# The front of a cell-and-feed-forward kernel: a weight converted in ten pieces instead of sixteen, in smaller steps, in another written order

## Chip, core and metric

The kernel runs on one core of a Trainium2 chip, in one launch. The metric is the device time of that launch in microseconds. Three runs of the kernel before gave 463.89, 464.75 and 465.46 us; the median is 464.75 us.

## What is computed

Two blocks follow each other. The first is an mLSTM cell over 4 batches, 8 heads, 768 time steps and a head width of 40; the second is a feed-forward layer with an exact GELU on the 3072 x 320 matrix that the first one gives. The weights arrive in 64-bit floating point.

```python
for t in range(S):                                   # B, H, S, D = 4, 8, 768, 40
    m_new  = maximum(f_gate[t] + m, i_gate[t])
    f_stab = exp(f_gate[t] + m - m_new); i_stab = exp(i_gate[t] - m_new); m = m_new
    C = f_stab * C + i_stab * outer(v[t], k[t])
    n = f_stab * n + i_stab * k[t]
    y[t] = sigmoid(o_gate[t]) * (C @ q[t]) / maximum(abs(n . q[t]), 1)
x = y, laid out as (B*S, H*D)                        # 3072 x 320
h = x @ w_in                                         # w_in 320 x 2048, w_out 2048 x 320
out = (0.5 * h * (1 + erf(h / sqrt(2)))) @ w_out
```

## The kernel before

The 768 steps are cut into 6 chunks of 128. Inside a chunk the cell is written with matrix products: scores (`ps`, L539), weighted by a mask of decays `W`, times the values (`ph`, L657), plus what the state carries in (`pf`, L577 and L582). A chunk has four batches. The feed-forward part takes a chunk's 512 rows at a time: an up product (`pu`, L806 and L812 for chunk 0), GELU on ScalarE (L816), a down product (`po`, L1044 for chunk 0).

The engines run independently and each in the order in which the program issues its instructions. That order is written out by hand in strings. `FRONT` covers the start: chunk 0's cell (small letters), chunk 1's cell (capitals), and chunk 0's feed-forward part. `play` walks through the string word by word; the letter picks a step, the number is its argument. The steps that matter below are these:

- `O n` and `L n` issue loads on SP's queue: `O` the values `vb` and the output gate `ob` of batch n, `L` its keys and queries. Batch numbers run on over the chunks, so `O4` is chunk 1's first batch. `B n` loads a mask tile `W` from DRAM, `M` masks it on GpSimd (L441), `w`/`W` takes its exponential on ScalarE (L467).
- `t`/`T` transposes keys and queries on TensorE (L517); ScalarE copies them out (L520). `T` also weighs chunk 1's values on VectorE (`vw`, L526), which reads `vb`. `c`/`C` is the carried part; for chunk 0 it begins with `vw` on VectorE, then products into a `pf` bank, then a copy of the state on ScalarE (L592). `s`/`S` are the scores and their weighting on VectorE (L542), `v`/`V` the values' products into a `ph` bank, `y`/`Y` the finishing on VectorE (L674 to L679, with a copy `y_rest`, L686), which reads `ph`. `pf` and `ph` share two PSUM banks, tag `h`. `x`/`X` transposes the result for the feed-forward part (L697).
- `A` and `U` are chunk 0's up products for its first and its second half of the rows, four steps each. The second `A` needs weight pieces 3 and 4.
- `F` is one of 16 rows of the down product; row f needs `w_out[:, f, :]`.
- `k n` issues n products that nobody reads, `I n` has the next bank filled with n such products first.
- `K` and `J` convert one piece of a weight from 64 to 32 bits. `K` (`conv_one`): VectorE L371 takes the exponent, ScalarE L373 and L374 turn it into a power of two, VectorE L376 and L378 build the significand. `J` (`conv_two`): VectorE L385 puts in the sign, L388 multiplies and writes the weight; then `fetch(i + 4)` issues the load of the piece four further on into the buffer `bits` of which there are four, so that this load waits in SP's queue until L385 has read the old piece. Ten pieces of 512 columns are `w_in`, then come 16 pieces of 320 columns, one for each row of `w_out`.
- `E` and `N` compute the gates of chunk 1 and of chunks 2 to 5: scans on VectorE, a store of `M` to DRAM on SP, a transpose on TensorE, differences and exponentials.

After `FRONT` come chunk 1's up and down products and so on (`up`, L949 and L960; `down_steps`, L1065), which the change does not touch.

Of the kernel before, what the change touches and what calls it, by code (L numbers as in the profile page):

```python
# [9 lines left out]
F32 = mybir.dt.float32  # L10
F32R = mybir.dt.float32r
BF16 = mybir.dt.bfloat16
U32 = mybir.dt.uint32
# [3 lines left out]
P = 128  # L17
# [8 lines left out]


FRONT = """
    I2 O0 g0 L0 P0 L1 E k1 t0 P1 P2 k7 w0 N k2 w1 O1 K L2 Q s0 O3 w2 q D
    k2 d P3 t1 w3 c0 L3 J v0 t2 K K y0 s1 I7 v1 I8 O2 J g1 L4 I5 c1 K I1  # L30
    I2 y1 s2 x0 t3 B4 O4 B5 g2 J x1 s3 v2 c2 L5 y2 H T0 x2 G0 v3 g3 c3 K y3
    M1 J L6 J A x3 M0 K W0 O7 K A O6 O5 J M2 W1 S0 C0 K J J T1 U U
    K L7 V0 K T2 r J J A G2 K G1 Y0 W2 S1 K M3 C1 A J S2 J K W3 K
    V1 C2 Y1 T3 J J U U S3 V2 K K J G3 J Y2 C3 X0 K V3 J K F J F
    K K B8 F J K F F J K F F F R0 X1 J J K F J F K X2 F J
    K F J Y3 K F R1 e J F Z B9 B10 F X3 R2 Z R3 F p"""
DOWN = """
    F Z M0 Z W0 F M1 L3 W1 S0 C0 M2 F B3 K2 F G1 h0 Q2 D3 G2 V0 K3 Z W2 F Q3 V1 M3 G0 Z F G3 W3 S2 C2 h2 F Y0 F V2
    F Y1 X0 N Y2 F R0 V3 F X1 F Y3 j X2 R1 F R2 X3 R3 F"""
# [3 lines left out]
def kernel(  # L43
# [16 lines left out]
    nc = tc.nc  # L60

    B, H, S, D = q.shape
    L = P
    NCH = S // L
# [4 lines left out]
    DM = H * D  # L69
    DFF = moe_w_in.shape[1]  # L70
    NF = DFF // P
# [6 lines left out]
    WP = 512  # L78
# [5 lines left out]
    raw = ctx.enter_context(tc.tile_pool(name="raw", bufs=2))  # L84
# [14 lines left out]
    w_out = const.tile([P, NF, DM], F32, name="w_out", tag="w_out")  # L99
# [28 lines left out]
    M_d = dram.tile([NCH - 1, BH, L], F32, name="M_d")  # L128
# [3 lines left out]
    def out_of(n):  # L132
        return ob[n % NLD].rearrange("p (h d) -> p h d", d=D)
# [6 lines left out]
    def swapped(c, b):  # L140

        return c > 1 and b % 2 == 1

    def load(n, first=0, end=4):

        if n >= NCH * B:
            return
        c, b = divmod(n, B)
        for src, dst in ((q, qb), (k, kb), (v, vb), (o_gate, None))[first:end]:
            if dst and swapped(c, b):  # L150
                x, to = src[b, :, c * L:(c + 1) * L, :].rearrange("h p d -> p h d"), dst[turn_of(n)][:, :, 0:D]
# [3 lines left out]
            nc.sync.dma_start(out=dst[turn_of(n)][:, :, 0:D] if dst else out_of(n),  # L155
                              in_=src[b, :, c * L:(c + 1) * L, :].rearrange("h p d -> p h d"))
# [19 lines left out]
    def turn_of(n):  # L176

        return n % NLD if n < 2 * B else (n - 2 * B) % NQ
# [35 lines left out]
    a = gates.tile([BH, NCH, L], F32, name="a")  # L214
    M = gates.tile([BH, NCH, L], F32, name="M")
# [58 lines left out]

    def decays_of(e0, e1, g0, g1):

        e, g = slice(e0, e1), slice(g0, g1)
        nc.vector.tensor_tensor(out=ew[:, e], in0=a[:, e], in1=M[:, e, L - 1:L].to_broadcast([BH, e1 - e0, L]),
                                op=OP.subtract)
        nc.vector.tensor_tensor(out=gg[:, g], in0=m0[:, g0 + 1:g1 + 1].unsqueeze(2).to_broadcast([BH, g1 - g0, L]),  # L280
                                in1=M[:, g0 + 1:g1 + 1], op=OP.subtract)
        nc.scalar.activation(out=ew[:, e], in_=ew[:, e], func=AF.Exp)
        nc.scalar.activation(out=gg[:, g], in_=gg[:, g], func=AF.Exp)

    def decays_turned(e0, e1, g0, g1):
        e, g = slice(e0, e1), slice(g0, g1)
        gates_turned((ew[:, e], ewT[:, e]), (gg[:, g], gT[:, g]))
# [21 lines left out]

    def second_gates():  # L310
        gates_of(1, 2)
        nc.sync.dma_start(out=M_d[0], in_=M[:, 1])
        gates_turned((a[:, 1:2], aT[:, 1:2]))
        decays_of(0, 2, 0, 1)

    def later_gates():
        gates_of(2, NCH)
        nc.sync.dma_start(out=M_d[1:].rearrange("c p l -> p c l"), in_=M[:, 2:])
        gates_turned((a[:, 2:], aT[:, 2:]))
        decays_of(2, NCH - 1, 1, NCH - 1)  # L320


    w_src = {}
    for name, w in (("in", moe_w_in), ("out", moe_w_out)):
        rows, cols = w.shape
# [3 lines left out]
    pieces = []  # L329
# [13 lines left out]
    def in_tile(i, x):  # L343

        return w_all[i // 4 * 5 + (2 if x == NX else x + (i % 4) // 2 * 3)]
    for f in range(NF):
        pieces.append(([w_src["out"][f * P:(f + 1) * P, :]], w_out[:, f, :]))
    bits, sig, pow2 = {}, {}, {}

    def fetch(i):  # L350
# [11 lines left out]
    def conv_one(i):  # L362

        if i < len(pieces):
            n = bits[i].shape[1]
            lo, hi = bits[i][:, :, 0], bits[i][:, :, 1]
            s = sig[i] = raw.tile([P, WP], F32, name="sig", tag="sig")[:, 0:n]
            p = pow2[i] = raw.tile([P, WP], F32, name="pow", tag="pow")[:, 0:n]
            su, pu = s.bitcast(U32), p.bitcast(U32)
# [8 lines left out]
            nc.vector.scalar_tensor_tensor(out=s, in0=lo, scalar=2.0 ** -32, in1=su, op0=OP.mult, op1=OP.add)  # L378

    def conv_two(i):  # L380

        if i < len(pieces):
            hi, p = bits.pop(i)[:, :, 1], pow2.pop(i)
            pu = p.bitcast(U32)
            nc.vector.scalar_tensor_tensor(out=pu, in0=hi, scalar=0x80000000, in1=pu,  # L385
                                           op0=OP.bitwise_and, op1=OP.bitwise_or)
            dst, s = pieces[i][1], sig.pop(i)
            nc.vector.scalar_tensor_tensor(out=dst, in0=s, scalar=2.0 ** -20, in1=p, op0=OP.mult, op1=OP.mult)  # L388
            fetch(i + NB)

# [733 lines left out]
    def in_turn(steps):  # L1124
        todo = list(steps)
        return lambda: todo.pop(0)() if todo else None
# [9 lines left out]
    def first_blocks():  # L1136

        copy_chunk(2, range(1))
        for r in (32, 96):
# [2 lines left out]

    first_g = Hidden(False)
    n_pieces = range(len(pieces))
    steps = dict(P=fetch, L=lambda n: load(n, 0, 2), O=lambda n: load(n, 2, 4), B=load_M, E=second_gates, N=later_gates,
                 I=keep_clock, k=warm, D=lambda: decays_turned(0, 2, 0, 1), Q=lambda: decays_turned(2, NCH - 1, 1, NCH - 1),
                 d=lambda: decays_last(0, 1), q=lambda: decays_last(1, NCH - 1), r=halves_out, p=halves_back,
                 A=in_turn(first_up_steps(0)), U=in_turn(first_up_steps(1)), e=first_blocks, F=in_turn(first_down_steps(first_g)),
                 K=in_turn(lambda i=i: conv_one(i) for i in n_pieces), H=products_begin,
                 J=in_turn(lambda i=i: conv_two(i) for i in n_pieces), Z=split_weight)  # L1150
    steps |= cell_steps(0, "mwgtscvyx") | cell_steps(1, "MWGTSCVYXR")
    play(FRONT, steps)
    for c in range(1, NCH):
# [6 lines left out]
        steps = cell_steps(c + 1, "MWGTscVYXRLKQDCBSjh", g)  # L1160
# [36 lines left out]
```

## Time and profile before

| | us |
|---|---|
| median of three runs | 464.75 |
| profiled execution, its own time | 465.24 |
| its span in the profile | 463.2 |
| TensorE busy | 452.3 (98%) |
| VectorE busy | 336.7 (73%) |
| ScalarE busy | 253.0 (55%) |
| GpSimd busy | 79.0 (17%) |
| chunk 0's first up product starts / chunk 0's down product starts / chunk 1's up product starts | 40.8 / 93.5 / 128.8 |

The 2.0 us between the span and the execution's own time lie around the program. Times in the text below are those of the profile, from the start of the span. In a line of the timeline the first number is the start, the second the duration, and where idle time came before an instruction it stands in brackets with what ended it. VectorE's instructions overlap a little, so the step from one start to the next is what counts in a sum; it is up to 0.1 us shorter than the duration.

### The profile page before, as it was taken

How to read it: one execution, taken by the hardware profiler on the slowest of the kernel's cores; microseconds unless marked ns; L12 is line 12 of the kernel's file. 1: busy time of each engine (PE TensorE's matmuls, PEld its weight loads, DVE VectorE, ACT ScalarE, POOL GpSimd, SP SyncE). 2: the span in 40 equal slices, each digit the busy share in tenths (PEclk: the TensorE clock that was granted, in tenths of full speed). 3: DMA queues.
4: the chain of work that ended last, by engine and by line, in shares of the span. 5: the costliest groups of instructions: out<-in, count | busy, mean ns of one | idle time of the engine just before them, and what ended most of it. 6: DMA issues, size and time to landing. Idle time of an engine off the chain costs nothing.

```text
span 463.2 us, 13002 instructions
## 1 busy us (share of the span) xinstructions
PE 452.3 (98%) x5348; PEld 400.5 (86%) x5348; DVE 336.7 (73%) x737; ACT 253.0 (55%) x545; POOL 79.0 (17%) x120
## 2 busy tenths in 40 slices
PE   8899999999999999999998999999999999999996
PEld 7687888867788899988898998899998899988996
DVE  7899879798868996746577654587664685699950
ACT  6986999854354784203694113594123594257701
POOL 3002120000020232300443200353301411200000
PEclk9999999999999999999999999999999999999999
DMA  9997993268777650057972056973049960210001
GB/s 168 203 215 184 199 224 105 64 135 226 111 201 153 120 98 5 24 115 149 200 124 33 11 118 139 208 112 61 1 87 172 164 106 3 79 38 0 1 1 57
DMA packets 174875, 51.11 MB, mean 110 GB/s; under 512 B 154752, under 2 KB 168352, under 8 KB 174816
## 3 DMA queue, kind: packets, MB, share of 16 engines
q1 hardware_dynamic: 174496, 49.95, 52.9%
q8 instruction: 42, 0.69, 0.6%
q10 hardware_dynamic: 320, 0.33, 0.2%
q14 instruction: 17, 0.14, 0.1%
HBM read 45.47 MB, written 10.03 MB: 120 GB/s over the span
## 4 chain that ended last, share of the span: by engine, by line
PE 89%; DVE 4%; DMA 2%; SPq 1%; POOL 1%; issue 1%; ACT 0%; DVEq 0%; POOLq 0%
PE po L1065 25%; PE pu L949 23%; PE po L1044 7%; PE pu L806 6%; PE pu L960 6%; PE po L919 6%; PE ph L657 4%; PE ps L555 3%; PE pu L812 2%; PE px L697 2%; PE pf L610 1%; PE ps L539 1%; SPq L155 1%; PE pf L577 1%; PE pt L517 1%
## 5 line engine op out<-in xcount | busy, mean ns | idle before, releaser
L1065 PE MATMUL po<-w_out,g 128*128 128x160 f32 x512 | 76.2, 303 | 0.0
L964 ACT ACTIVATE g<-pu 128x512 f32<-128x512 f32 x64 | 32.2, 618 | 77.4 <-PE pu L960 77.4
L1065 PEld LDWEIGHTS po<-w_out,g 128*128 128x128 f32 x512 | 70.3, 190 | 2.2 <-ACT g L964 1.3
L467 ACT ACTIVATE W<-W,aT 128x128 f32<-128x128 f32 x128 | 39.2, 389 | 2.1 <-POOL W L441 2.0
L949 PE MATMUL pu<-x_hi,w_in_hi 128*128 128x512 f32 x160 | 39.0, 387 | 0.0
L441 POOL TENSOR_SCALAR_AFFINE_SELECT W<-W 128x1024 f32<-128x1024 f32 (+2 forms) x20 | 25.0, 1258 | 79.1 <-DMA W<-M_d 70.4
L949 PE MATMUL pu<-x_lo,w_in_lo 128*128 128x512 f32 x160 | 37.8, 379 | 0.0
L1065 PE MATMUL po<-w_sums,sums 128*128 128x160 f32 x256 | 36.9, 302 | 0.0
L1065 PEld LDWEIGHTS po<-w_sums,sums 128*128 128x128 f32 x256 | 35.0, 190 | 0.4
L1044 PE MATMUL po<-w_out,g 128*128 128x320 f32 x128 | 35.2, 433 | 0.0
L686 ACT COPY y_rest<-ob 128x128 f32<-128x128 f32 x16 | 4.8, 298 | 55.4 <-DVE ob L679 29.2
L949 PEld LDWEIGHTS pu<-x_hi,w_in_hi 128*128 128x128 f32 x160 | 29.5, 189 | 5.7 <-ACT g L964 1.3
L949 PEld LDWEIGHTS pu<-x_lo,w_in_lo 128*128 128x128 f32 x160 | 30.2, 189 | 4.3
L526 POOL TENSOR_TENSOR vw<-vb,ewT 128x328 f32<-128x328 f32 x12 | 9.2, 780 | 138.4 <-DMA vb<-in_v_dram 99.2
L1044 PEld LDWEIGHTS po<-w_out,g 128*128 128x128 f32 x128 | 24.0, 190 | 9.6
L949 PE MATMUL pu<-x_all,w_mid 128*128 128x512 f32 x80 | 30.3, 379 | 0.0
L949 PE MATMUL pu<-x_all,w_in_mid 128*128 128x512 f32 x80 | 30.3, 379 | 0.0
L806 PE MATMUL pu<-first_x,w_in 128*128 128x256 f32 x128 | 28.9, 381 | 0.0
L793 DVE TENSOR_TENSOR sums<-g 128x512 f32<-128x512 f32 x16 | 13.6, 853 | 18.3 <-ACT g L964 18.3
L806 PEld LDWEIGHTS pu<-first_x,w_in 128*128 128x128 f32 x128 | 23.8, 190 | 3.3 <-DVE w_in L388 0.2
L765 DVE TENSOR_TENSOR w_in_mid<-w_in_hi,w_in_lo 128x512 fp32r<-128x512 f32 x20 | 13.7, 686 | 16.5 <-PE pu L949 16.5
L561 DVE TENSOR_TENSOR W<-ps,W 128x256 f32<-128x256 f32 (+1 forms) x48 | 17.9, 413 | 10.7 <-PE ps L555 9.0
(196 smaller groups left out, 963.2 us busy)
## 6 DMA issues: line engine op xcount, KB each, us to landing
W<-M_d SPq DMA_DIRECT2D x16, 512.0 KB, 5.6
bits<-in_moe_w_in_dram SPq DMA_DIRECT2D x20, 256.0 KB, 4.5
bits<-in_moe_w_out_dram SPq DMA_DIRECT2D x16, 320.0 KB, 3.2
blocks<-kq_d SPq DMA_DIRECT2D x32, 128.0 KB, 3.3
ob<-in_o_gate_dram SPq DMA_DIRECT2D x24, 160.0 KB, 4.4
out_dram<-o_sb SPq DMA_DIRECT2D x36, 80.0 KB, 2.0
kq_d<-in_k_dram SPq DMA_DIRECT2D x32, 80.0 KB, 2.5
kq_d<-in_q_dram SPq DMA_DIRECT2D x32, 80.0 KB, 2.5
```

What stands on the lines that cost most here:

```text
L441: nc.gpsimd.affine_select(out=x, in_=x, compare_op=OP.is_ge, fill=1.0e30, base=base, pattern=[[0, H], [1, x.shape[2]]], channel_multiplier=-1)
L467: nc.scalar.activation(out=W[n][:, h, :], in_=src, func=AF.Exp, scale=-1.0, bias=aT[:, self.c, r:r + 1])
L555: nc.tensor.matmul(ps[i][hip][halves[x ^ i], p, t], kT[i][r, p, halves[x]], qT[i][r, p, t], start=True, stop=True)
L561: nc.vector.tensor_tensor(out=w[r, :, t], in0=ps[i][hip][r, :, t], in1=w[r, :, t], op=OP.mult)
L657: nc.tensor.matmul(ph[r, h, :], Pm[:, h, r], vb[turn_of(n)][:, h, :], start=True, stop=True)
L806: nc.tensor.matmul(banks[-1][e][:, i - i0, :], in_tile(i, x)[:, e, i % 2 * P:(i % 2 + 1) * P], first_x[:, x, t0:t1], start=(x == 0 and i = ...
L919: nc.tensor.matmul(in_pairs(po[t]), x[:, t * L:(t + 1) * L], in_turns(w), start=(f, k) == first, stop=(f, k) == last, skip_group_check=True)
L949: nc.tensor.matmul(in_pairs(pus[i][e]), w[k][:, e, i * P:(i + 1) * P], in_turns(x[:, k, :]), start=(n == 0 and k == 0), stop=False, skip_g ...
L960: nc.tensor.matmul(in_pairs(pu[e]), w[r, i // 2, i % 2 * P:(i % 2 + 1) * P], in_turns(x[r, NX, :]), start=False, stop=(n == 2), skip_group ...
L964: nc.scalar.activation(out=g.t[:, HF * e + i, :], in_=pu[e], func=AF.Gelu, scale=4097.0)
L1044: nc.tensor.matmul(po[b], g.t[:, f, b * L:(b + 1) * L], w_out[:, f, :], start=(f == 0), stop=(f == NF - 1))
L1065: nc.tensor.matmul(bank[k][:, t, :], lhs(j, t), rhs(j), start=(first and t == 0 and j == 0), stop=(t == 1 and j == HF - 1), skip_group_che ...
```

## The change

`w_out` is converted as one run of 5120 columns, cut into ten pieces of 512 instead of sixteen of 320. A piece then holds parts of two or three rows of `w_out`, and its load is issued as two or three DMAs, 24 in all instead of 16. `K` keeps L371 and the two ScalarE operations; L376 and L378 become a step `b` (`conv_sig`). `J` keeps L385; L388 and the fetch become a step `f` (`conv_out`). `E` and `N` are taken apart into `a` (scans), `o` (store), `n` (transpose) and `l` (decays). The string is written anew:

```diff
 FRONT = """
-    I2 O0 g0 L0 P0 L1 E k1 t0 P1 P2 k7 w0 N k2 w1 O1 K L2 Q s0 O3 w2 q D
-    k2 d P3 t1 w3 c0 L3 J v0 t2 K K y0 s1 I7 v1 I8 O2 J g1 L4 I5 c1 K I1
-    I2 y1 s2 x0 t3 B4 O4 B5 g2 J x1 s3 v2 c2 L5 y2 H T0 x2 G0 v3 g3 c3 K y3
-    M1 J L6 J A x3 M0 K W0 O7 K A O6 O5 J M2 W1 S0 C0 K J J T1 U U
-    K L7 V0 K T2 r J J A G2 K G1 Y0 W2 S1 K M3 C1 A J S2 J K W3 K
-    V1 C2 Y1 T3 J J U U S3 V2 K K J G3 J Y2 C3 X0 K V3 J K F J F
-    K K B8 F J K F F J K F F F R0 X1 J J K F J F K X2 F J
-    K F J Y3 K F R1 e J F Z B9 B10 F X3 R2 Z R3 F p"""
+    I2 O0 g0 L0 P0 L1 E l0,2,0,1 t0 o1,2 P1 w0 a2,6 P2 k7 o2,6 n l2,5,1,5 k3 w1 O1 K b L2 Q s0 O3 w2 q D k2 d
+    P3 t1 w3 c0 b L3 J f v0 t2 K b y0 s1 K I7 O2 J f v1 g1 L4 I5 c1 K b I1 I2 y1 s2 x0 t3 B4 J x1 f s3 v2 v3
+    O4 B5 g2 c2 L5 y2 H T0 x2 G0 g3 c3 K b J f y3 L6 J M1 f A x3 M0 K b W0 O7 K b A O6 O5 J f M2 W1 S0 C0 K b
+    J f J f T1 U U K b L7 V0 K b T2 r J f J f A G2 K b G1 Y0 W2 S1 K b M3 J C1 A f S2 J f K b K b V1 C2 Y1 T3
+    J f W3 J U U S3 V2 K f b K b J f G3 J f Y2 C3 X0 K b V3 J K b F J f f F K b K b B8 F J f F F J f F F F R0
+    X1 F F X2 F F Y3 F R1 e F F Z B9 X3 Z B10 R2 R3 F p"""
...
-    for f in range(NF):
-        pieces.append(([w_src["out"][f * P:(f + 1) * P, :]], w_out[:, f, :]))
+    cuts = sorted({*range(0, NF * DM, DM), *range(0, NF * DM + 1, WP)})
+    for n in range(0, NF * DM, WP):
+        rows = [(c // DM, c % DM, d - c) for c, d in zip(cuts, cuts[1:]) if n <= c < n + WP]
+        pieces.append(([w_src["out"][f * P:(f + 1) * P, 2 * c:2 * (c + w)] for f, c, w in rows],
+                       w_out.rearrange("p f d -> p (f d)")[:, n:n + WP]))
...
+    def conv_sig(i):
+        if i < len(pieces):
+            lo, hi = bits[i][:, :, 0], bits[i][:, :, 1]
+            s = sig[i] = raw.tile([P, WP], F32, name="sig", tag="sig")[:, 0:bits[i].shape[1]]
+            su = s.bitcast(U32)
             nc.vector.tensor_scalar(out=su, in0=hi, scalar1=0xFFFFF, scalar2=0x100000,
                                     op0=OP.bitwise_and, op1=OP.bitwise_or)
             nc.vector.scalar_tensor_tensor(out=s, in0=lo, scalar=2.0 ** -32, in1=su, op0=OP.mult, op1=OP.add)
...
+    def conv_out(i):
+        if i < len(pieces):
+            dst, s, p = pieces[i][1], sig.pop(i), pow2.pop(i)
+            bits.pop(i)
             nc.vector.scalar_tensor_tensor(out=dst, in0=s, scalar=2.0 ** -20, in1=p, op0=OP.mult, op1=OP.mult)
             fetch(i + NB)
```

In the third line of the old string and the second and third of the new one, three moves stand out: `v3` goes from behind `T0 x2` to right behind `v2`; `O4 B5` goes from ahead of the third `J` to behind that piece's `f` and behind `s3 v2 v3`; and one `K` goes behind `s1`.

More of the change, by code (lines that the diff above doesn't have):

```diff
@@ L311, in second_gates, with store_M, later_turned @@
         gates_of(1, 2)
-        nc.sync.dma_start(out=M_d[0], in_=M[:, 1])
         gates_turned((a[:, 1:2], aT[:, 1:2]))
[L314 to L318, printed above, removed]
+    def store_M(c0, c1):
+        nc.sync.dma_start(out=M_d[c0 - 1:c1 - 1].rearrange("c p l -> p c l"), in_=M[:, c0:c1])
+    def later_turned():
         gates_turned((a[:, 2:], aT[:, 2:]))
-        decays_of(2, NCH - 1, 1, NCH - 1)
     w_src = {}
@@ L364, in conv_one @@
         if i < len(pieces):
[L365 to L369, printed above, removed]
+            hi = bits[i][:, :, 1]
+            p = pow2[i] = raw.tile([P, WP], F32, name="pow", tag="pow")[:, 0:bits[i].shape[1]]
+            pu = p.bitcast(U32)
             nc.vector.tensor_scalar(out=pu, in0=hi, scalar1=20, scalar2=0x7FF,
@@ L382, in conv_two @@
         if i < len(pieces):
-            hi, p = bits.pop(i)[:, :, 1], pow2.pop(i)
-            pu = p.bitcast(U32)
+            hi, pu = bits[i][:, :, 1], pow2[i].bitcast(U32)
             nc.vector.scalar_tensor_tensor(out=pu, in0=hi, scalar=0x80000000, in1=pu,
                                            op0=OP.bitwise_and, op1=OP.bitwise_or)
-            dst, s = pieces[i][1], sig.pop(i)
+    def conv_out(i):
+        if i < len(pieces):
+            dst, s, p = pieces[i][1], sig.pop(i), pow2.pop(i)
+            bits.pop(i)
             nc.vector.scalar_tensor_tensor(out=dst, in0=s, scalar=2.0 ** -20, in1=p, op0=OP.mult, op1=OP.mult)
@@ L1144 @@
     n_pieces = range(len(pieces))
-    steps = dict(P=fetch, L=lambda n: load(n, 0, 2), O=lambda n: load(n, 2, 4), B=load_M, E=second_gates, N=later_gates,
+    steps = dict(P=fetch, L=lambda n: load(n, 0, 2), O=lambda n: load(n, 2, 4), B=load_M, E=second_gates, n=later_turned,
+                 a=gates_of, o=store_M, l=decays_of,
                  I=keep_clock, k=warm, D=lambda: decays_turned(0, 2, 0, 1), Q=lambda: decays_turned(2, NCH - 1, 1, NCH - 1),
@@ L1149 @@
                  K=in_turn(lambda i=i: conv_one(i) for i in n_pieces), H=products_begin,
-                 J=in_turn(lambda i=i: conv_two(i) for i in n_pieces), Z=split_weight)
+                 J=in_turn(lambda i=i: conv_two(i) for i in n_pieces), b=in_turn(lambda i=i: conv_sig(i) for i in n_pieces),
+                 f=in_turn(lambda i=i: conv_out(i) for i in n_pieces), Z=split_weight)
     steps |= cell_steps(0, "mwgtscvyx") | cell_steps(1, "MWGTSCVYXR")
```

## The prediction

> **What bounds the kernel now.** I read the page first: TensorE is busy for 98% of the span, VectorE for 73%. Then I asked for the busy time by stretch, to see where TensorE's missing 2% lie.
>
> ```profile
> PE 452.3 (98%) x5348; PEld 400.5 (86%) x5348; DVE 336.7 (73%) x737; ACT 253.0 (55%) x545; POOL 79.0 (17%) x120
> ```
> ```profile
> 46.00:68.00 22.00, 22.00 (x219) 18.50 (x219) 17.15 (x33) 21.72 (x41) 3.91 (x4) 1.00 1.02 224
> 68.00:72.00 4.00, 4.00 (x59) 3.31 (x58) 3.83 (x11) 3.97 (x8) 0.37 (x1) 1.00 0.56 162
> 72.00:92.00 20.00, 20.00 (x306) 17.41 (x304) 16.56 (x43) 18.57 (x38) 0.00 (x0) 1.00 0.25 70
> 92.00:94.00 2.00, 1.56 (x68) 1.17 (x67) 1.91 (x6) 1.94 (x4) 0.00 (x0) 1.00 0.00 0
> 94.00:129.00 35.00, 35.00 (x138) 24.87 (x136) 29.80 (x80) 16.59 (x32) 1.04 (x1) 1.00 0.77 165
> ```
>
> The columns are the stretch, its length, then busy time with instruction counts of PE, PEld, DVE, ACT and POOL. From 46 us on TensorE idles 0.44 us up to 129 us, at full clock (1.00), and the down product runs evenly: in the chain of waits 64 of L1044's matmuls take 17.42 us and 40 take 10.77, 0.27 each. So a shift of the point where this unbroken stretch begins comes out at the end one to one, and nothing saved on another engine behind that point comes out at all. Who sets the point? The waits of PEld between 46 and 130 us name one edge, and the timeline shows it:
>
> ```profile
> PEld pu L806 <- DVE w_in L388: 0.2, 1, 0.2
> ```
> ```profile
> 38.84 0.49 DVE L526 TENSOR_TENSOR vw<-vb,ewT 128x328 f32<-128x328 f32 x1
> ...
> 40.44 1.46 DVE L378 SCALAR_TENSOR_TENSOR sig<-bits,sig 128x512 f32<-128x512 uint32 x1
> ...
> 45.56 0.69 DVE L388 SCALAR_TENSOR_TENSOR w_in<-sig,pow 128x512 f32<-128x512 f32 x1
> ...
> 45.88 3.72 PE L806 MATMUL pu<-first_x,w_in 128*128 128x256 f32 x16
> ```
>
> The second A starts at 45.88 and its second matmul needs weight piece 4, which VectorE finishes at 46.25. VectorE has worked almost without a pause since 3.5 us, so **the kernel's length is set by when VectorE finishes piece 4**; after that TensorE sets it. Two more things of this stretch matter: when loads are issued, and how long they take to land.
>
> ```profile
> 30.56 1.62 SPq L191 DMA_DIRECT2D W<-M_d  x1
> 32.27 0.39 SPq L155 DMA_DIRECT2D vb<-in_v_dram  x1
> 32.76 0.52 SPq L155 DMA_DIRECT2D ob<-in_o_gate_dram  x1
> 33.33 2.96 SPq L191 DMA_DIRECT2D W<-M_d  x1
> 36.39 1.68 SPq L359 DMA_DIRECT2D bits<-in_moe_w_in_dram  x2
> ```
> ```profile
> 40.19 2.66 POOL L441 TENSOR_SCALAR_AFFINE_SELECT W<-W 128x1024 f32<-128x1024 f32 x2 [34.90 <-DMA W<-M_d]
> ```
> ```profile
> blocks<-in_q_dram SPq DMA_DIRECT2D x1, 160.0 KB, 4.2
> ```
> ```profile
> qb<-in_q_dram SPq DMA_DIRECT2D x1, 160.0 KB, 5.6
> ```
> ```profile
> vb<-in_v_dram SPq DMA_DIRECT2D x1, 160.0 KB, 5.1
> ```
>
> The last three are the DMA issues of short windows: at 29.50 and 45.38 a 160 KB load right behind two loads of a piece, and O4's `vb` at 32.27.
>
> **The change part by part.** I add to the profiled execution, 465.24 us (span 463.2 and 2.04 around it), and carry the shift to the median, 464.75.
>
> *Ten pieces.* By start-to-start steps a 320-column piece costs VectorE 0.23+0.35+0.41+0.52+0.41 = 1.92 us and a 512-column one 0.33+0.46+0.61+0.72+0.61 = 2.73; 16 x 1.92 - 10 x 2.73 = 3.4 us saved. ScalarE: 16 x (0.557+0.562) - 10 x (0.720+0.722) = 3.5 us saved. All of it lies behind 69.9 us, where the first w_out piece begins, beside an unbroken TensorE: 0 on the path. Per piece ScalarE takes 0.32 longer; four come before the last GELU of chunk 0 ends (90.66), which makes it some 92, and the down product starts at 93.5: covered with 1.5 us to spare, beyond which it would count in full. All conversion ends after about the sixth F row (some 107 us instead of 125); each row has its columns early. The 8 more DMAs cost SP 8 x 0.33 = 2.6 us of issue in a stretch in which it spends 28 us on eight issues, waiting for L385: 0.
>
> *Gates in two parts.* VectorE's, ScalarE's and SP's orders stay what they were (scans, store, transpose copy, differences, exponentials, then piece 0). Only `w0`'s products go ahead of seven unread ones, so ScalarE's wait of 1.37 us at 11.42 ends, but it then waits for the differences, as now, until 13.76. 0. One unread product less before `t0`, one more before `w1`: 0.
>
> *Conversion in smaller steps, up to piece 4.* The same VectorE instructions stand before the end of piece 4 in both orders, so only its pauses can change. One `K` (L371) behind `s1` brings W(s1) forward by 0.3, but its ScalarE pair and the table load behind it move to 27.5, `g1` ends at 30.8 instead of 29.5 and `y1` starts 0.2 late. The pause ahead of the last scores (0.49, ScalarE's copies of `t3`) stays. So `y2` runs from 37.26 instead of 37.14: +0.1.
>
> *v3 forward.* It needs W(s3), done at 36.85, so it fills TensorE's 0.72 us pause at 37.28. But now `v2` and `v3` hold both banks of tag `h`, and `c2` must wait until `y2` has read its own, 38.0: about when `v3` is through. `c2`, `T0`, `x2`, `c3` would give the first A at 40.6, against 40.78. Small either way, as piece 4 decides.
>
> *O4 and B5 behind the third piece's fetch.* Here I see the cost. That fetch waits for L385 of piece 2, at 34.4 (33.63 to 34.31 now). SP, free at 32.2, stands still for 2.2 us, then issues two loads of 256 KB (1.2 us), and `vb` of O4 goes out at 35.65 instead of 32.27. `T0`'s `vw` reads it and stands on VectorE at 38.96, ahead of `c3`'s `vw`, pieces 3 and 4 and `y3`. Landing: 4.2 to 5.6 us after the issue by the two nearest rows, both a 160 KB load behind two pieces; I take 5.0, near the row of this same load, hence 40.65. VectorE waits 40.65 - 38.96 = 1.7 us (0.9 to 2.3). Queued behind it: everything to piece 4, and `c3` on TensorE.
>
> *GpSimd's masks.* The L378 at 40.44 took 1.46 instead of 0.69 while the first mask ran: 0.77 us of the present path. B5 now goes out at some 36.6 and lands some 2.8 us after `vb`, near 43.4; the masks then meet piece 3's L385 or L388. I take 0.7 again (0 if they fall into `y3`, whose input is in PSUM and which was not stretched at 41.83; 1.5 if both masks hit).
>
> The Trainium skill (SBUF — State Buffer, "Who interferes with whom") calls this port an exclusive lock that a VectorE instruction with two SBUF inputs shares with a GpSimd one that reads SBUF; by it the whole mask is the price, 1.2 us, if the mask starts first, and the sum would be 0.5 us higher; this row shows 0.77.
>
> *The sum.* Without either, piece 4 would end at 46.25 - 0.77 + 0.1 = 45.6. With them 45.6 + 1.7 + 0.7 = 48.0, a shift of 1.75, say 1.7. The later order changes (`W3` behind `T3`, the last `X3` one DMA earlier, the rest of F) leave TensorE's list as it was: 0. Profiled execution 466.9, **median 466.4**. Ends: 45.6 + 0.9 = 46.5 (+0.25) and 45.6 + 2.3 + 1.5 = 49.4 (+3.15), so 465.0 to 467.9.
>
> **The rivals.**
>
> *The load is in time; nothing changes.* If `vb` lands by 38.96, 3.3 us after its issue, the wait is 0 and only the mask's 0.7 stays: 45.6 + 0.7 = 46.3, that is 464.8. For it: early loads on an empty queue land that fast (`vb` issued at 1.63 has landed by 4.5). Against: the B mask tile ahead is 512 KB and lands at 36.5. The Trainium skill (DMA: Bandwidth & Descriptors, "Anatomy of one DMA") gives 2.0 us plus bytes over 436 GB/s, an estimate of 2.4 us for 160 KB, by which the load is in time; every load of that size between 20 and 50 us took 4.2 us or more.
>
> *Faster: the small steps win what they can.* The load is in time, the masks fall into `y3`, and the second A starts as soon as TensorE is there: 45.6, or -0.65; the lighter engines also remove TensorE's two pauses behind (0.44 at 92.9; 16 matmuls of L539 at 68.7 take 1.43 instead of 0.89 us). -0.65 - 0.44 - 0.54 = -1.6: 463.1. Against it: the profile puts both pauses down to issue, to no engine that is made lighter.
>
> *Slower by more: the banks.* If `c3`'s bank is the one that `v3` holds, `c3` on TensorE waits for `y3`, which stands behind piece 3's conversion: `y3` has read at some 45.7, `c3` and the first A (4.8 us) then push the second A to 51.4, +5.4: 470.2. Against it: `c2`'s bank is free by then, its state being copied at 39.2.
>
> **How the numbers follow.** Forecast 0.58, load in time 0.21, faster 0.13, banks 0.08. A measurement here tells 0.3% (1.4 us) from no change. Of the forecast's spread (+0.25 to +3.15, centre 1.7) some two thirds lie above 1.4: 0.40, and with the banks 0.48 slower. Its lower third and the load in time give 0.18 + 0.21 = 0.39 the same; 0.13 faster. The range takes in both near rivals partly and the top end with a little more: 463.9 to 468.3.
>
> **What would show it.** In the profile after: SP issues `vb` of O4 at 35 to 36 us, behind the two `bits` loads; L526 on VectorE shows a wait of 1 to 2 us for the DMA of `vb` near 39; the masks start near 43 and one VectorE instruction of piece 3 is stretched; the second A starts near 47.5 and the down product near 95.3, the last with no pause between its rows; VectorE's busy time falls by about 3.4 us and ScalarE's by 3.5. I am wrong if `vw` does not wait, if the second A starts before 46, if TensorE pauses between 50 and 129, or if the down product waits for a `w_out` piece.

## The result

| | before | after |
|---|---|---|
| median, same chip, six runs each | 465.23 us (463.89 to 466.88) | 470.01 us (469.09 to 471.81) |
| profiled execution / its span | 465.24 / 463.2 | 470.9 / 469.1 |

The ratio is 1.0099, with a 95% interval of 1.0071 to 1.0126: slower by some 4.8 us. The prediction said slower, by 1.7 us, with an upper end of 468.3; the time lies above that end. The page of the kernel after begins:

```profile
PE 454.0 (97%) x5348; PEld 401.9 (86%) x5348; DVE 334.7 (71%) x707; ACT 249.8 (53%) x533; POOL 80.3 (17%) x120
```

VectorE is busy for 2.0 us less (forecast 3.4) and ScalarE for 3.2 us less (forecast 3.5), TensorE for 1.7 us more (its granted clock was 0.79 between 248 and 256 us). The stretches again, columns as before:

```profile
46.00:68.00 22.00, 21.79 (x222) 18.21 (x219) 16.71 (x30) 20.98 (x39) 4.61 (x4) 1.00 0.96 221
68.00:72.00 4.00, 3.75 (x30) 2.68 (x29) 3.93 (x8) 3.29 (x7) 0.00 (x0) 1.00 0.48 67
72.00:92.00 20.00, 19.30 (x239) 16.70 (x238) 19.32 (x46) 18.97 (x36) 0.00 (x0) 1.00 0.35 109
92.00:94.00 2.00, 2.00 (x99) 1.82 (x97) 1.22 (x3) 1.99 (x4) 0.00 (x0) 1.00 0.98 290
94.00:98.00 4.00, 2.24 (x84) 1.78 (x79) 3.93 (x10) 3.41 (x6) 0.00 (x0) 1.00 0.34 104
98.00:133.00 35.00, 35.00 (x138) 24.86 (x136) 21.75 (x49) 11.45 (x20) 1.03 (x1) 1.00 0.68 126
```

TensorE now has holes where it had none, 0.25 us between 68 and 72 and 0.70 between 72 and 92, and just ahead of the down product it stands for 1.76 us instead of 0.44. (The 0.21 that is missing between 46 and 68 is the second `A`, which waits for piece 4.) The waits between 37 and 130 us name the holes (total, count, longest):

```profile
PE ph L663 <- issue: 1.8, 1, 1.8
...
DVE vw L532 <- DMA vb<-in_v_dram: 1.3, 1, 1.3
PE pf L583 <- DVE vw L532: 1.2, 1, 1.2
...
PE pf L583 <- DVE state L603: 0.7, 1, 0.7
...
PE ps L545 <- ACT kT L526: 0.2, 1, 0.2
```

The second and the third are the forecast wait and its echo on TensorE. The first was 0.44 us before; the last two are new. Set side by side at points of TensorE's fixed order, the two profiles give this account:

| TensorE starts | before | after | shift | added since the row above |
|---|---|---|---|---|
| S0 (L539, now L545) | 50.49 | 52.05 | 1.56 | 1.56: forecast as 1.7 |
| C1 (L577, now L583) | 70.24 | 72.26 | 2.02 | 0.46 |
| C2 | 77.78 | 80.58 | 2.80 | 0.78 |
| down product (L1044, now L1050) | 93.53 | 97.65 | 4.12 | 1.32 |
| up product of chunk 1 | 128.83 | 132.96 | 4.13 | 0.01 |

From there to the end this profile takes 336.1 us, that of before 334.4. The same stretch took 332.5 to 336.2 us in the profiles of all the kernels told of here, without order, so I read nothing from it; the medians, 4.8 us apart, leave 0.7 us for it.

**The forecast part** is there line by line (issue on SP, then VectorE, GpSimd and TensorE):

```profile
35.29 0.38 SPq L153 DMA_DIRECT2D vb<-in_v_dram  x1
```
```profile
40.30 0.50 DVE L532 TENSOR_TENSOR vw<-vb,ewT 128x328 f32<-128x328 f32 x1 [1.32 <-DMA vb<-in_v_dram]
...
43.25 1.47 DVE L394 SCALAR_TENSOR_TENSOR w_in<-sig,pow 128x512 f32<-128x512 f32 x1
...
47.12 0.69 DVE L394 SCALAR_TENSOR_TENSOR w_in<-sig,pow 128x512 f32<-128x512 f32 x1
```

The load goes out at 35.29, 5.0 us later `vw` may start, GpSimd's mask begins at 43.08 and stretches one instruction of piece 3, and piece 4 is done at 47.81, where I had 48.0.

**The first unforecast part** lies on VectorE and GpSimd, 64 to 67 us. After, and then before:

```profile
63.69 1.39 DVE L532 TENSOR_TENSOR vw<-vb,ewT 128x328 f32<-128x328 f32 x1
65.00 1.02 DVE L367 TENSOR_SCALAR pow<-bits 128x512 uint32<-128x512 uint32 x1
65.93 1.25 DVE L378 TENSOR_SCALAR sig<-bits 128x512 uint32<-128x512 uint32 x1
```
```profile
63.27 1.45 POOL L447 TENSOR_SCALAR_AFFINE_SELECT W<-W 128x1024 f32<-128x1024 f32 x1 [8.01 <-ACT qT L526]
64.78 2.12 POOL L1146 MEMSET blocks<- 32x1024 f32 x2
```
```profile
65.45 1.46 DVE L378 SCALAR_TENSOR_TENSOR sig<-bits,sig 128x512 f32<-128x512 uint32 x1
66.84 0.49 DVE L526 TENSOR_TENSOR vw<-vb,ewT 128x328 f32<-128x328 f32 x1
67.25 0.68 DVE L385 SCALAR_TENSOR_TENSOR pow<-bits,pow 128x512 uint32<-128x512 uint32 x1
```
```profile
65.18 1.19 POOL L441 TENSOR_SCALAR_AFFINE_SELECT W<-W 128x1024 f32<-128x1024 f32 x1 [8.23 <-DVE pow L371]
66.43 1.94 POOL L1140 MEMSET blocks<- 32x1024 f32 x2
```

Before, the fourth mask stretched one instruction (1.46 for 0.69) and the two memsets that follow it on GpSimd met `vw` and L385, which kept their times. After, the mask stretches `vw` (1.39 for 0.49) and the memsets meet two TENSOR_SCALARs, which take 1.02 and 1.25 instead of 0.42 each: 2.3 us in all instead of 0.8. VectorE is then late for ScalarE, which waits 0.67 us for L367 ahead of its copies of T2's keys, and for the state that C2 reads. Here is the last addition to that state and C2's first product, before and then after:

```profile
75.89 0.32 DVE L597 TENSOR_TENSOR state<-state,pf 128x164 f32<-128x164 f32 x1
...
77.78 0.67 PE L577 MATMUL pf<-vw,kb 128*64 128x41 f32 x16
```
```profile
80.10 0.33 DVE L603 TENSOR_TENSOR state<-state,pf 128x164 f32<-128x164 f32 x1
...
80.58 0.67 PE L583 MATMUL pf<-vw,kb 128*64 128x41 f32 x16 [0.70 <-DVE state L603]
```

**The second** is the pause inside V3, ahead of the down product, which both profiles put down to "issue":

```profile
93.31 0.28 PE L657 MATMUL ph<-v,W 128*32 128x41 f32 x8 [0.44 <-issue]
```
```profile
97.44 0.28 PE L663 MATMUL ph<-v,W 128*32 128x41 f32 x7 [1.76 <-issue]
```

### The profile page after: what moved, and what is told of

Its sections match the earlier page's. It is cut to its first block, busy times and chain, and to the rows that moved or that the text cites. A ratio compares the mean times of both kernels' runs of the same rounds, so it can differ in the third digit from the quotient of the medians.

```text
span 469.1 us, 12974 instructions
## 1 busy us (share of the span) xinstructions
PE 454.0 (97%) x5348; PEld 401.9 (86%) x5348; DVE 334.7 (71%) x707; ACT 249.8 (53%) x533; POOL 80.3 (17%) x120
## 4 chain that ended last, share of the span: by engine, by line
PE 75%; DVE 8%; DMA 6%; ACT 4%; SPq 2%; issue 2%; POOL 2%; POOLq 0%; DVEq 0%; ACTq 0%
PE pu L955 22%; PE po L1071 21%; PE po L1050 7%; PE po L925 6%; PE pu L966 5%; PE ph L663 3%; PE pu L812 2%; PE ps L561 2%; DMA vb<-in_v_dram 2%; PE px L703 2%; ACT W L473 1%; PE pf L616 1%; SPq L153 1%; POOL W L447 1%; DMA W<-M_d 1%
## 5 line engine op out<-in xcount | busy, mean ns | idle before, releaser
L1050 PE MATMUL po<-w_out,g 128*128 128x320 f32 x128 | 35.2, 433 | 0.0
L1050 PEld LDWEIGHTS po<-w_out,g 128*128 128x128 f32 x128 | 24.0, 190 | 9.6
```

The source lines that it names most:

```text
L1050: nc.tensor.matmul(po[b], g.t[:, f, b * L:(b + 1) * L], w_out[:, f, :], start=(f == 0), stop=(f == NF - 1))
```

## The experiments

The table compares all of them; each ratio is taken against runs of the kernel before on the same chip. "S0 to down" is the time from TensorE's S0 to the start of the down product. A shift of TensorE ahead of S0 drops out of it, but a late S0 gives the other engines more lead (b_load). "C2" and "V3" are the two pauses.

| kernel | ratio to before | C2 | V3 | S0 to down |
|---|---|---|---|---|
| before | | 0 | 0.44 | 43.04 |
| after | 1.0099 [1.0071, 1.0126] | 0.70 | 1.76 | 45.60 |
| b_load | 1.0034 [1.0013, 1.0055] | 0 | 0.22 | 42.48 |
| a_load | 1.0054 [1.0007, 1.0100] | 0.70 | 1.49 | 44.75 |
| b_ten | 1.0050 [1.0032, 1.0068] | 0 | 1.75 | 44.71 |
| b_B8 | 1.0006 [0.9986, 1.0025] | 0 | 0.63 | 43.07 |
| b_more | 1.0091 [1.0060, 1.0121] | 0 | 2.02 | 44.29 |
| b_hold | 1.0020 [0.9998, 1.0042] | 0 | under 0.15 | 42.77 |
| a_mem | 1.0054 [1.0034, 1.0074] | 0 | 1.26 | 43.66 |
| a_hold | 1.0062 [1.0042, 1.0081] | 0.71 | 0.76 | 44.59 |
| a_c1 | one run, 465.96 beside 463.71 us | 0 | 1.40 | 43.91 |
| a_fix | 0.9993 [0.9979, 1.0007] | 0 | 0.31 | 42.58 |
| a_best | 1.0057 [1.0035, 1.0079] | 0 | 0.71 | 45.60 |
| a_after4 | 0.9994 [0.9978, 1.0011] | 0 | 0.39 | 43.08 |

### b_load: the kernel before, O4 and B5 moved alone

```diff
-t3 B4 O4 B5 g2 J x1 s3 v2 c2
+t3 B4 g2 J x1 s3 v2 O4 B5 c2
```

> The kernel before with one move: O4 and B5 go from ahead of the third J to behind it (and behind s3 and v2), nothing else. Theory A (the late load of vb is what shifts piece 4): vb of O4 is issued at about 35.5 instead of 32.3, T0's vw on VectorE waits 1.0 to 1.8 us for it near 39, the second A starts its second matmul at 47.3 to 48.0 instead of 46.2, and chunk 0's down product starts 1.0 to 1.8 us later than in the kernel before (93.5). Rival (the shift comes from the split steps or from v3): vw does not wait or the wait is swallowed, and the down product starts within 0.4 us of 93.5.

```profile
40.31 0.50 DVE L526 TENSOR_TENSOR vw<-vb,ewT 128x328 f32<-128x328 f32 x1 [1.39 <-DMA vb<-in_v_dram]
```

The wait is 1.39 us, the second A stands until 48.14, and the down product starts at 94.81, 1.28 later than before. The move alone makes the wait and costs the time, a ratio of 1.0034. That step of the prediction holds.

### a_load: the kernel after, O4 and B5 ahead of the third J again

```diff
-t3 B4 J x1 f s3 v2 v3 O4 B5 g2 c2
+t3 B4 O4 B5 J x1 f s3 v2 v3 g2 c2
```

> The changed kernel with that move alone taken back: O4 and B5 stand ahead of the third J again. Theory A: vb is issued near 32.5, vw does not wait, piece 4 is done at 45.6 to 46.4 instead of 47.8, and the start of the down product (97.65 in the changed kernel) comes 1.3 to 3 us earlier, the upper end if the GpSimd collisions of 63 to 67 us move away with it. Rival: the load is only the first of several late things, and the down product still starts later than 97.0, because the masks or the state of chunk 1 take its place.

```profile
38.86 0.49 DVE L532 TENSOR_TENSOR vw<-vb,ewT 128x328 f32<-128x328 f32 x1
...
40.47 1.56 DVE L380 SCALAR_TENSOR_TENSOR sig<-bits,sig 128x512 f32<-128x512 uint32 x1
...
41.95 1.57 DVE L386 SCALAR_TENSOR_TENSOR pow<-bits,pow 128x512 uint32<-128x512 uint32 x1
```

`vw` no longer waits, but now both early masks meet a piece, at 0.87 and 0.88 us, so the second A ends only 0.5 earlier. The waits of C2 and V3 stay. The down product starts at 96.33, 1.3 earlier, at the low end of what was expected; 2.8 of the 4.1 us stay. By the ratio about half of the loss stays, with a wide interval.

### b_ten: the kernel before, with the ten pieces alone

```diff
-    for f in range(NF):
-        pieces.append(([w_src["out"][f * P:(f + 1) * P, :]], w_out[:, f, :]))
+    cuts = ...   # the ten runs of 512 columns, as in the change
```

> The kernel before with w_out in ten pieces of 512 columns and nothing else (its ten K, J pairs left over do nothing). Theory A: up to the first up products nothing changes; from 70 us on a K or J takes longer (2.73 instead of 1.92 us of VectorE for a piece), so chunk 1's states come later and a wait of up to 0.7 us may show ahead of C2 near 78; the down product starts at 93.4 to 94.6. Rival (longer pieces are the main loss behind 68 us): it starts at 95.5 or later. What the prediction said: 93.5, no change.

```profile
95.00 0.28 PE L660 MATMUL ph<-v,W 128*32 128x41 f32 x8 [1.75 <-issue]
```
```profile
90.00:92.00 2.00, 2.00 (x100) 1.79 (x96) 1.82 (x5) 1.99 (x5) 0.00 (x0) 1.00 0.92 310
```

With the old order and nothing else changed, the down product starts 1.68 us late, at 95.21, between the two cases expected; C2 does not wait. Of the 1.68, 1.31 is the pause inside V3. The other 0.37 lies ahead of C3: the longer pieces make ScalarE late (it copies T3's queries at 88.35 instead of 86.70), and the weight load of S3 waits 0.50 us for that copy. This is the edit that I had put at 0. What differs from before at that point is the traffic: DMA share 0.92 between 90 and 92 us, where it was 0.03. Two pieces are now five loads, issued from 88.0 to 90.3 us (the two loads of before went out at 85.5 and 86.9) and landing until 95.0, and in the trace TensorE's next 16 KB of instructions come in their midst, from 92.07 to 93.56. The page lists the queue that they come in (packets, MB, share of the DMA engines' time):

```profile
q8 instruction: 42, 0.69, 0.6%
```

That they are TensorE's is inferred. Each kernel has 42 packets of 16 KB in this queue, against 10,696 matmuls and weight loads, 255 to a packet; all other instructions of the span are some 2,300. The pause stands at a fixed place of TensorE's list: behind 56 of V3's 64 products in the kernels with the old order, behind 57 in those with the new one. And behind 30 us the 14 profiles told of here have 39 pauses of TensorE that are put down to "issue": all stand among products of 41 columns, and each ends 1.1 to 1.7 us after such a packet has landed (those in V3 1.1 to 1.5). The profile itself says only "issue". b_B8, b_more, b_hold and a_hold test what traffic does to it.

### b_B8: the kernel before, the 512 KB load of B8 moved to 87.3 us

```diff
-U U S3 V2 ... K K B8 F J K F
+U U S3 B8 V2 ... K K F J K F
```

> The kernel before with the 512 KB load of B8 issued right behind the scores S3 (near 88 us) instead of behind the second F (near 103), so that data moves while TensorE's next instructions are loaded near 91 us. Theory B (the pause inside V3 is TensorE waiting for its instructions, and data traffic stretches it): the pause of 0.44 us inside V3 grows to 1 to 2 us, the 16 KB instruction load near 91 us takes longer or starts later, and the down product starts 0.6 to 1.6 us later. Rival (the pause in the changed kernel has another cause, such as VectorE's W): it stays between 0.3 and 0.6 us.

```profile
93.51 0.28 PE L657 MATMUL ph<-v,W 128*32 128x41 f32 x8 [0.63 <-issue]
```
```profile
90.00:92.00 2.00, 2.00 (x93) 1.82 (x79) 2.00 (x5) 0.89 (x3) 0.00 (x0) 1.00 0.36 111
```

The pause grew by 0.19 only, and the time did not change. By what was expected that speaks for the rival. But the load was nearly through when the packet came: the DMA share was 0.36, not 0.92. So the test was too weak, and the next makes it stronger.

### b_more: the kernel before, with four more loads at that time

```diff
+    spare = dram.tile([4, P, WP], U32, name="spare")
+    def spare_loads():
+        for n in range(4):
+            nc.sync.dma_start(out=spare[n], in_=w_src["out"][n * P:(n + 1) * P, 0:WP])
...
-T3 J J U U S3
+T3 J J z U U S3
```

> Left as it is: the kernel before, 16 pieces, its own order. Added: four loads of 256 KB from w_out to a scratch place in DRAM, issued right behind the two fetches that follow T3 (at 87.4 us before), which nobody reads. TensorE's instructions are those of the kernel before up to the down product. Theory (TensorE's next 16 KB of instructions come through the same DMA engines as the data, and the loads that are under way at 91 us hold them up): the instruction packet takes 1.3 us or more instead of 1.10 or starts late, the pause inside V3 is 1.2 to 1.9 us instead of 0.44, and the down product starts at 94.3 to 95.0 instead of 93.5. Rival (the longer pause has to do with the other program, not with traffic): pause 0.2 to 0.6, down product at 93.4 to 93.7. Second rival (the number of DMAs counts, not their bytes; these are four, the ten-piece kernels have five small ones): pause in between, 0.6 to 1.2.

```profile
98.94 0.28 PE L663 MATMUL ph<-v,W 128*32 128x41 f32 x8 [2.02 <-issue]
```
```profile
94.00:96.00 2.00, 2.00 (x95) 1.85 (x83) 2.00 (x5) 1.07 (x3) 0.00 (x0) 1.00 0.89 240
```

Four loads that nobody reads, and the pause is 2.02 us: traffic alone makes it, with 16 pieces. All starts here are some 4 us later than before because TensorE ran at a granted clock of 0.50 from 16 to 24 us in this profiled execution; S0 to the down product leaves that out. The ratio is larger than the pause explains, but six of the seven runs had a mean granted clock of 0.985 to 0.996, where three of 32 runs of before had 0.996 or less on that chip. The seventh, at 0.999, took 465.44 us, 1.2 more than the median of before there (464.26), which is what S0 to the down product shows. Why the clock was lower in the other six stays open.

### b_hold: ten pieces, two of their fetches held back

```diff
-T3 J J U U S3 V2 K K J G3 J            # these two J fetch pieces 16 and 17
+T3 J J U U S3 V2 K K z16 z17 J G3 J    # z: a memset of one column of bits on VectorE, then the fetch
```

> The kernel before with the ten w_out pieces alone, but the loads of pieces 16 and 17 held back until VectorE has begun two more pieces (a memset of one column on VectorE ahead of each load, behind the K K that follow V2): they go out at 94 to 95 us instead of 88 to 90.5, so nothing is loaded while TensorE fetches its instructions at 91 to 93.5. Theory (traffic holds the instructions up): the pause inside V3 falls from 1.75 to 0.2 to 0.7, and the down product starts at 93.8 to 94.3 instead of 95.2 (0.26 of the ten pieces' delay ahead of S3 and 0.1 behind it stay). Time 465.5 to 466.5 beside 467.7. Rival (not the traffic at that time): pause 1.5 to 1.9, down product at 95.0 to 95.4, time 467.5.

```profile
93.06 1.16 PE L663 MATMUL ph<-v,W 128*32 128x41 f32 x64
```
```profile
90.00:92.00 2.00, 2.00 (x98) 1.82 (x96) 1.83 (x3) 1.99 (x4) 0.00 (x0) 1.00 0.05 12
```

The same ten pieces with nothing loaded at 90 to 92 us: V3's 64 products run through without a pause, and from S0 to the down product it takes 42.77 us instead of b_ten's 44.71. (S0 itself is 0.9 late here, as both early masks met piece 4: 1.31 and 1.46 us for 0.42 and 0.69.) The rival that the other program makes the pause is out: taken away and put in, the traffic decides. Whether the number of the DMAs or their bytes count is not separated as well, since both go together here; the rival on the number had 0.6 to 1.2 us for b_more, which shows 2.02.

The packets' own records show more; their start is counted from the first product of C3, so that TensorE's place in its list is the same in every row. The DMA share is that of the two us in which C3 starts:

| kernel | DMA share, 90 to 92 us (b_more 94 to 96) | packet starts behind C3 | takes | pause |
|---|---|---|---|---|
| before | 0.03 | 0.36 | 1.10 | 0.44 |
| b_hold | 0.05 | 0.34 | 1.01 | under 0.15 |
| b_B8 | 0.36 | 0.69 | 1.07 | 0.63 |
| b_ten | 0.92 | 1.23 | 1.49 | 1.75 |
| b_more | 0.89 | 2.20 | 1.02 | 2.02 |

The packet begins up to 1.8 us later. That it stands in line behind data is an inference from this order; no view shows it waiting. How long it takes does not follow the traffic: 1.02 us in b_more, but 1.46 in a_best, where the share was 0.06.

### a_mem: the kernel after, the memsets on VectorE

```diff
     def first_blocks():
...
-            nc.gpsimd.memset(blocks[r:r + 32], 0.0)
+            nc.vector.memset(blocks[r:r + 32], 0.0)
```

> The kernel after with one change: the two memsets of blocks in first_blocks are issued on VectorE, late (behind R1), instead of on GpSimd, which did them at 64.8 to 66.9 us right behind the fourth mask. Theory (they held VectorE up): L367 at 65.00 and L378 at 65.93 take 0.42 again instead of 1.02 and 1.25, VectorE is 1.4 us earlier from there, the 0.24 us wait ahead of the scores of T2 is gone, and the state is added 1.2 to 1.4 us earlier, so that the 0.70 us wait ahead of C2 is gone too; the down product starts at 96.2 to 96.9 instead of 97.65 (more if the instruction packet is then held up less). Rival (VectorE is not what those waits are for, or the lock is taken by the mask alone): L367 and L378 still take 1.0 or more, the waits stay, down product at 97.4 to 97.8.

```profile
63.89 1.38 DVE L532 TENSOR_TENSOR vw<-vb,ewT 128x328 f32<-128x328 f32 x1
65.20 0.41 DVE L367 TENSOR_SCALAR pow<-bits 128x512 uint32<-128x512 uint32 x1
65.53 0.41 DVE L378 TENSOR_SCALAR sig<-bits 128x512 uint32<-128x512 uint32 x1
```

Both TENSOR_SCALARs have their 0.41 us again, and the waits ahead of T2's scores and of C2 are gone. The down product starts at 95.93 instead of 97.65, 0.3 earlier than expected, because V3's pause shrank too (1.26). A memset on GpSimd that nobody waited for was worth 1 us and more. `vw` is still stretched, by the mask.

### a_c1: the kernel after, C1 ahead of the eleventh J again

```diff
-M3 J C1 A f S2
+M3 C1 A J f S2
```

> The kernel after with C1 ahead of the eleventh J again (M3 C1 A J f S2), the memsets left on GpSimd. Theory (the order alone costs nothing: C2's wait comes from VectorE being late through the mask and the memsets): L603's last addition of the state, 80.43 us in the kernel after, comes 0.7 us earlier because L386 of that piece no longer stands ahead of it, and the wait ahead of C2 falls from 0.70 to 0.0 to 0.1, so either cure is enough; down product 0.6 to 0.8 earlier, at 96.8 to 97.1, if the pause inside V3 stays at 1.76. Rival (the state does not depend on J's place): wait 0.6 to 0.8, down product 97.4 to 97.8.

```profile
78.31 0.33 DVE L603 TENSOR_TENSOR state<-state,pf 128x164 f32<-128x164 f32 x1
78.55 0.69 DVE L386 SCALAR_TENSOR_TENSOR pow<-bits,pow 128x512 uint32<-128x512 uint32 x1
```

C2 does not wait. The addition to the state begins 3.69 us after the weighting of S1 (74.62) instead of 4.29 (75.81 to 80.10): L386 ahead of it was worth 0.6. In this run the collisions were also lighter and the front earlier, so the down product's 95.5 (expected 96.8 to 97.1) is not this edit's alone, and a single run leaves its time open. The state is done at 78.64 and C2 starts 0.14 later (0.15 in the kernel after); so with L386 still ahead of the state C2 would have started 0.6 later, nearly all of the 0.70. a_mem takes away as much by its own edit: either cure is enough.

### a_hold: the kernel after, fetches 16 and 17 held back alone

The same edit as in b_hold, behind the `K b` that follow `V2`.

> The kernel after with the loads of pieces 16 and 17 alone held back, as in the kernel before with ten pieces: they go out behind the K b that follow V2 (some 97 us) instead of at 90.8 to 93.1. Theory (traffic holds TensorE's instructions up): pause inside V3 0.2 to 0.7 instead of 1.76, everything up to V3 as in the kernel after (S3 at 91.4 to 91.7), down product at 96.1 to 96.7 instead of 97.65, time 468.4 to 469.2 on the scale of 470.0 for the kernel after and 465.2 for the kernel before, a ratio of 1.007 to 1.0085. Rival (in this kernel the pause has another source): pause 1.5 or more, ratio 1.009 to 1.011.

```profile
PE ph L666 <- issue: 0.8, 1, 0.8
...
PE pf L586 <- DVE state L606: 0.7, 1, 0.7
```

The pause falls from 1.76 to 0.76, slightly above the range expected, and C2's wait stays, as it should. The packet started 0.50 behind C3 but took 1.29 with a DMA share of 0.05, so some of its spread is not traffic. The down product is 1.6 earlier; 1.0 of that is the pause and 0.6 is ahead of S0, where `vw` happened to wait 0.72 instead of 1.32; that also puts the ratio under the one expected.

### a_fix: four causes taken out together

a_load's and a_c1's orders, a_mem's memset and a_hold's fetches in the kernel after.

> The kernel after with four causes taken out together: O4 and B5 ahead of the third J again, the memsets of first_blocks on VectorE, C1 ahead of the eleventh J again, and the loads of pieces 16 and 17 held back on VectorE until behind the K b that follow V2. If these are all of what the change costs: no wait of vw at 38.9, no wait ahead of C2, pause inside V3 0.2 to 0.7, down product at 93.3 to 94.6 (both masks still meet VectorE at 40.5 to 43.5, worth up to 1.2 us on the second A), and a time within 1.0 us of the kernel before, 464.2 to 466.2. If something else of the change costs time: down product later than 95, time 467 or more.

The ratio is 0.9993 [0.9979, 1.0007]: the loss is gone within what these runs can tell (1.0 us under to 0.3 us over the kernel before), with ten pieces, smaller steps and `v3` forward all kept. So these four account for what the change cost; small costs and gains that cancel would not show. Its profile has the down product at 95.99, later than expected, but in that execution (465.96 us) the granted clock was low early on, as in b_more's:

```profile
16.00:24.00 8.00, 7.71 (x51) 6.23 (x47) 5.02 (x14) 5.88 (x18) 0.00 (x0) 0.57 0.97 184
```

Its second scores start 2.58 us late (26.57), and S0 to the down product takes 42.58, less than before.

### a_best and a_after4: can the front then be faster than before?

In a_fix the two early masks still met piece 4 (1.33 and 1.46 us for 0.42 and 0.69). a_best loads the second mask tile late, so that both masks run behind piece 4:

```diff
-t3 B4 O4 B5 J x1 ... c3 K b J f y3
+t3 B4 O4 J x1 ... c3 K b J f B5 y3
```

> The kernel after with the four cures (loads O4 in time, memsets on VectorE, C1 first, loads of pieces 16 and 17 held back) and B5 moved behind the f of piece 3, so that the two masks run at 47 to 50 us, behind piece 4, instead of at 40 to 42.5 beside pieces 3 and 4. If the masks are what holds piece 4 up there: L380 and L382 of piece 4 take 0.42 and 0.69, the waits ahead of the second A and inside it (0.36 and 0.56 us with the four cures alone) are gone, and the time is 0.6 to 1.0 us under that of the four cures alone: 463.2 to 463.8 where the kernel before has 464.3, ratio 0.997 to 0.9985. If the exponential W0 then waits for its mask: S0's weighting late, and the time 464.2 or more.

```profile
51.46 2.45 ACT L476 ACTIVATE W<-W,aT 128x128 f32<-128x128 f32 x8 [2.19 <-POOL W L450]
```
```profile
PE pu L815 <- DVE W L551: 1.2, 1, 1.2
```

Piece 4 was clean and the second A started at 45.41, but the exponential of W0 waited 2.19 us for its mask, S0's weighting came late, and U0 stood for 1.2 us: the second expectation came true, and the ratio is 1.0057, slower than before. a_after4 keeps the early load and holds the masks by GpSimd itself:

```diff
+i=lambda: nc.gpsimd.tensor_copy(out=seen, in_=pieces[4][1][:, 0:1])
...
-y3 L6 J M1 f A
+y3 L6 J f i M1 A
```

> The kernel after with the four cures (loads of O4 and B5 early, memsets on VectorE, C1 first, loads of pieces 16 and 17 held back), and GpSimd's masks M1 and M0 held until VectorE has finished weight piece 4 (a copy of one column of that piece on GpSimd ahead of M1; the mask tiles are loaded early). The masks then run at some 45.5 to 48 us. If it is only their timing that matters: no instruction of pieces 3 and 4 is stretched, the second A runs from 45.4 without a wait, pieces 5 and 6 are stretched instead, W0 has its mask before its exponential at 49.3, no wait of TensorE between 46 and 92, and a time of 463.2 to 463.9 where the kernel before has 464.3 (ratio 0.9975 to 0.9995). If pieces 5 and 6 are then late for S0's weighting, or W0 waits for GpSimd as in the version with B5 late: a pause ahead of U0 at 54, time 464.3 or more, ratio 1.000 or more.

```profile
46.00:68.00 22.00, 22.00 (x220) 18.69 (x220) 17.42 (x31) 21.72 (x42) 4.89 (x4) 1.00 0.91 217
68.00:92.00 24.00, 24.00 (x365) 20.52 (x364) 22.46 (x52) 23.72 (x44) 0.00 (x0) 1.00 0.29 90
92.00:94.00 2.00, 1.61 (x68) 1.31 (x68) 1.97 (x5) 1.43 (x3) 0.00 (x0) 1.00 0.00 0
```

Now TensorE has no gap from 46 to 92 us and the down product starts at 93.31, 0.22 ahead of before. The ratio, 0.9994 [0.9978, 1.0011], cannot show so little. From 46 us on TensorE has almost no gap in either, so there was little to win: a_best is slower than the kernel before, and a_after4 does not differ from it by anything measured.

## Why the prediction was right and wrong

- **O4 and B5 behind the third fetch: right.** The issue at 35.3, the landing 5.0 us later, the wait (1.32, forecast 1.7 with 0.9 to 2.3) and its echo one to one at S0 all came as worked out. b_load reproduces it alone. The 5.0 us are one draw, though: in a_hold the same load was issued at 35.28 and `vw` started at 39.68, 4.4 us later, with a wait of 0.72, under the lower end. The rival "the load is in time" is out. The formula that it took from the Trainium skill (DMA: Bandwidth & Descriptors, "Anatomy of one DMA") is fitted there to DMAs that GpSimd issues. These are issued by SP, and 160 KB took 5.0 us here where the formula's estimate was 2.4.
- **GpSimd's masks, piece 4: right.** One instruction of piece 3 was stretched by 0.78 (forecast 0.7). The Trainium skill (SBUF — State Buffer, "Who interferes with whom") would have charged the whole mask if it starts first. Here it started 0.17 us ahead of L394 and ran for 1.09 us, which leaves 0.92 at most; the row shows 0.78, so in this case rule and row nearly agree. The 0 for masks that fall into `y3` was wrong: only its first three instructions read PSUM, and in b_load the masks stretched two later ones (L679, 0.83 us for 0.49, and L686, 1.00 for 0.23).
- **Smaller steps up to piece 4, v3 forward, gates in two parts: right as far as a sum can tell.** 1.56 us at S0 against 1.7.
- **Ten pieces: wrong, and this is the largest of the steps put at 0.** I put it there because the work lay "beside an unbroken TensorE", and priced the added DMAs by SP's issue time alone. The loads of two pieces became five DMAs issued back to back and 1 MB instead of 640 KB, went out 2.5 us later, and fell on the place where TensorE stands for what seems to be its next instructions. In b_ten this cost 1.31 us, in the kernel after 1.32. I had checked ScalarE's longer pieces only against the last GELU; in b_ten they cost another 0.37 ahead of C3, through its copies for S3. The profile of before had the clue: the 0.44 us pause put down to "issue" in that very place, which I quoted in the rival "faster" and did not ask about.
- **The later order, put at 0 since TensorE's list stays: wrong by 1.2 us.** I never worked out VectorE's lead over TensorE. At C2 it was 1.57 us before (state done at 76.21, C2 at 77.78). In the kernel after the state is done at 80.43, 4.2 us later, while TensorE would have been there only 2.1 us later: 1.6 us are S0's shift, 1.6 more collisions with GpSimd at 64 to 67 us, 0.6 the L386 of the eleventh J ahead of the state, and 0.4 belongs to the ten pieces (L367, L378 and L380 of a 512-column piece take 1.40 us ahead of the state, those of a 320-column one 0.99). a_mem and a_c1 each remove the wait.
- **What I had named as a sign of being wrong came true:** TensorE pauses between 50 and 129. The rival on the banks did not occur; `c3` waited for `vw`, not for `y3`.

The sum had the right mechanism for the part it looked at: of the 4.12 us at the down product, 1.56 were forecast as 1.7. The other 2.56 belong to the two terms put at 0. It failed in the assumption that an engine without idle time in one profile stays so in the next.

## What to carry to other kernels

An engine that never waits is covered by leads, and each lead has a size: before putting an edit at nothing, take the time between a helper's finish and the bottleneck's need at every hand-over behind it, and compare it with what the edit adds there. When instructions change places, ask which of them now stand beside GpSimd's work, even beside a memset that nothing waits for. And look at a pause put down to "issue" on the bottleneck: here each such pause ended shortly after a packet of instructions, and bulk loads ahead of it made it longer.

## What the runs showed of the hardware

- By count and by time TensorE's instructions come in 16 KB packets through the same DMA engines as data (inferred, see b_ten). Where the DMA share around C3's start was 0.06 or less, the packet that comes then cost 0 to 0.76 us of TensorE's time (seven profiles); at 0.36 it cost 0.63 (one), at 0.89 to 0.98 it cost 1.26 to 2.02 (six). The Trainium skill (Runtime: NRT & Kernel Launch, "Instruction fetch mechanics") says that crossing such a block is "mostly hidden". By count the trace agrees: two to four of the 42 packets of a profile have a pause behind them (counted behind 30 us). Those that do all meet products of 41 columns; V3's 64 of them run through in 1.16 us.
- GpSimd's memset stretched TENSOR_SCALAR (0.42 to 1.02 and 1.25 us) and left TENSOR_TENSOR and SCALAR_TENSOR_TENSOR alone (0.49, 0.68); its mask, which reads SBUF, stretched these too (0.49 to 1.39, 0.69 to 1.47). The Trainium skill (SBUF — State Buffer, "Who interferes with whom") says so: instructions with two SBUF inputs contend with GpSimd's reads, not with its mere writes, while `tensor_scalar` in a two-port mode takes the whole pair. The trace agrees; no view shows the mode itself.
- In two of the profiled executions TensorE's granted clock was 0.50 to 0.58 from 16 to 24 us (one product `pm` of 512 columns 0.63 us instead of 0.38), which cost 2.6 and 4.1 us at the front. In b_more the runs with a lower mean clock were the longer ones.
